# Down projection of a fused transformer block: two halves of an output row accumulated side by side, so that consecutive matmuls name the same stationary tile

## The chip, the cores and the metric

The kernel runs on one core of one Trainium2 chip. The metric is the device time of one execution in microseconds (us). Several executions of each kernel are timed, and medians are given with the lowest and highest run. Executions can fall into a slower state with a lower granted clock; every run on record here is marked as of the fast state (mean granted clock 0.994 to 1.000), so nothing here compares runs of different states.

## The reference

The reference computes one adaptive-layernorm block: linear attention with a residual, then a SwiGLU feed-forward network with a residual. What matters here is its last line, and in it the product with `w_down`.

```python
# x: 1 x 2048 x 1024 (bf16), w_gate and w_up: 1024 x 3584, w_down: 3584 x 1024
def _B_ref(x, w_gate, w_up, w_down):
    g = _silu(x @ w_gate)
    u = x @ w_up
    return g * u @ w_down
...
h = _layernorm(x, axis=-1) * (1 + cb) + sb
x = x + gb * _B_ref(h, B_w_gate, B_w_up, B_w_down)
```

## The kernel before

TensorE (PE) writes its sums to PSUM, which this kernel uses as 8 banks; ScalarE (ACT) and VectorE (DVE) take them out of the banks again, which is called evacuation below. A small scheduler records every operation through a helper and works out the semaphore waits from the buffers that each operation reads and writes. For PSUM it does so by bank. All instructions therefore carry the helper's line number, L178, in the profile, and one reads it by tile names.

The 2048 rows are worked on in four chunks of 512. Each chunk first computes `AT` (3584 x 512, as 28 tiles of 128 partitions), which is the product of gate and up. Then comes the down projection. For each of the four groups of 128 rows (a "row" below), each half of 512 output columns is one sum over the 28 tiles:

```python
# PS: PSUM, 8 banks of 512 fp32 columns. WD(ft): tile ft of w_down (128 x 1024), resident in SBUF.
for j in range(4):
    st = 4 * ch + j
    for nh in range(2):                                  # the two halves of a row of output
        bank = 4 + y_ctr[0] % 2
        i = y_ctr[0] % 2
        y_ctr[0] += 1
        last = (st == NST - 1 and nh == 1)
        parts = [(0, 384, bank), (384, 512, 6)] if last else [(0, 512, bank)]
        for (c0, c1, pb) in parts:
            for ft in range(NFT):                        # NFT = 28
                P.pe("matmul", out=PS[:, pb, c0:c1], lhsT=AT[:, ft, j * 128:(j + 1) * 128],
                     rhs=WD(ft)[:, nh * 512 + c0:nh * 512 + c1], start=(ft == 0), stop=(ft == NFT - 1))
            # evacuation: ACT copies the bank to ATT, DVE multiplies by GB_B, DVE adds to XRES, DMA out
            ...
```

`lhsT` is the stationary operand (128 x 128, loaded into the array by an LDWEIGHTS), and `rhs` is the moving one (512 columns streamed through). In this order the stationary tile changes with every matmul, and each tile of `AT` is loaded twice, 28 matmuls apart. One place in the kernel before already has pairs with equal stationary tiles:

```python
def m_mm(hg, banks):                                     # folds WO with the masked KV matrix
    for nh in range(2):
        ...
        P.pe("matmul", out=PS[:, bank, :], lhsT=KVT[:, hg, :], rhs=WO[:, hg, nh * 512:(nh + 1) * 512],
             start=True, stop=True)
```

## Time and profile before

| what | value | from |
|---|---|---|
| time, median of 3 | 841.77 us (841.69 to 842.76) | the timed runs |
| TensorE (PE) busy | 832.7 of 839.7 us, 99% | first part of the page |
| weight loads (PEld) busy | 384.4 us, 46% | first part of the page |
| first down stage (224 matmuls) | 401.84 - 353.49 = 48.35 us, 215.8 ns each | timeline |
| one weight load | 98 ns | groups by shape |

The first lines of the page. PE is TensorE's matmuls, PEld its weight loads, and PEclk the granted clock in tenths:

```profile
span 839.7 us, 10390 instructions
...
PE 832.7 (99%) x4291; PEld 384.4 (46%) x4291; DVE 296.6 (35%) x627; ACT 211.9 (25%) x363; POOL 39.7 (5%) x51
...
PEclk9999999999999999999999999999999999999999
```

There are as many loads as matmuls, 4291 of each: every matmul brings its own. A busy share of 99% doesn't yet say that PE can't go faster, because the ends of matmuls in the record are modelled and overlap the next. The chain of work that ended last is the stronger evidence. These are its last lines (start, length, what):

```profile
225.05 612.15 PE ps L178 x2877
837.23 0.30 DVE ut L178
837.55 0.22 DVE xres L178
```

For 612.15 us no matmul waited for anything, and the whole down projection lies inside that stretch. Now what sets the pace within it. First the groups by shape (count, busy us, mean ns of one, idle before), for the down projection and for the pairs that share `KVT`:

```profile
L178 PE MATMUL ps<-wd_a,at 128*128 128x512 bf16 x496 | 112.1, 379 | 0.0
L178 PE MATMUL ps<-wd_b,at 128*128 128x512 bf16 x372 | 85.3, 379 | 0.0
...
L178 PEld LDWEIGHTS ps<-wd_a,at 128*128 128x128 bf16 x528 | 51.1, 98 | 59.8
L178 PEld LDWEIGHTS ps<-wd_b,at 128*128 128x128 bf16 x396 | 38.3, 98 | 44.7
...
L178 PEld LDWEIGHTS ps<-wo,kvt 128*128 128x128 bf16 x16 | 1.5, 97 | 2.9 <-ACT mw L178 1.1 <-DVE kvt L178 0.4 <-DVE mw L178 0.2
```

The 379 ns of a matmul is its latency, not its pace. The pace is the distance of starts: 48.35 us / 224 = 215.8 ns. The Trainium skill, page "TensorE: Matmul & The Clock Gate", section "Phases on the wall clock", gives 512 columns at 2.4 GHz, 213 ns, plus a fixed 2.5 ns. The trace agrees, so matmuls already start at the pace that this formula gives for their columns alone, without a term for the load.

A timeline shows where a load is meanwhile. This is the end of the last row but one, and the start of the last row's first sum (start, length, engine, what, count):

```profile
823.79 1.24 PE L178 MATMUL ps<-wd_b,at 128*128 128x512 bf16 x5
824.01 0.53 PEld L178 LDWEIGHTS ps<-wd_b,at 128*128 128x128 bf16 x3
824.66 3.34 PEld L178 LDWEIGHTS ps<-wd_a,at 128*128 128x128 bf16 x16
824.87 3.62 PE L178 MATMUL ps<-wd_a,at 128*128 128x512 bf16 x16
825.15 0.60 ACT L178 ACTIVATE att<-ps 128x512 bf16<-128x512 f32 x1 [5.45 <-PE ps L178]
```

The 16 loads of `wd_a` matmuls start at 824.66, one matmul (0.21 us) before the first matmul that uses one. The 98 ns of a load lie under the 216 ns of the matmul before.

### The profile page before, as it was taken

How to read it: one execution, taken by the hardware profiler on the slowest of the kernel's cores; microseconds unless marked ns; L12 is line 12 of the kernel's file. 1: busy time of each engine (PE TensorE's matmuls, PEld its weight loads, DVE VectorE, ACT ScalarE, POOL GpSimd, SP SyncE). 2: the span in 40 equal slices, each digit the busy share in tenths (PEclk: the TensorE clock that was granted, in tenths of full speed). 3: DMA queues.
4: the chain of work that ended last, by engine and by line, in shares of the span. 5: the costliest groups of instructions: out<-in, count | busy, mean ns of one | idle time of the engine just before them, and what ended most of it. 6: DMA issues, size and time to landing. Idle time of an engine off the chain costs nothing.

```text
span 839.7 us, 10390 instructions
## 1 busy us (share of the span) xinstructions
PE 832.7 (99%) x4291; PEld 384.4 (46%) x4291; DVE 296.6 (35%) x627; ACT 211.9 (25%) x363; POOL 39.7 (5%) x51
## 2 busy tenths in 40 slices
PE   8999999999999999999999999999999999999998
PEld 4444444444444444444444444444444444444444
DVE  4677866656984211111121111122111112111111
ACT  5677763313332111101111111011111011111101
POOL 1000000000050000030000003000000300000000
PEclk9999999999999999999999999999999999999999
DMA  9792323756195895540355552035556203553000
GB/s 311 220 323 51 59 106 126 160 147 249 53 240 179 259 303 155 154 97 25 94 156 153 154 155 67 26 107 150 151 151 157 68 20 107 151 151 99 7 20 26
DMA packets 173391, 113.02 MB, mean 135 GB/s; under 512 B 32536, under 2 KB 156576, under 8 KB 173344
## 3 DMA queue, kind: packets, MB, share of 16 engines
q1 hardware_dynamic: 173344, 112.35, 47.2%
q8 instruction: 34, 0.56, 0.3%
q14 instruction: 13, 0.11, 0.0%
HBM read 100.67 MB, written 4.33 MB: 125 GB/s over the span
## 4 chain that ended last, share of the span: by engine, by line
PE 95%; SPq 2%; DMA 1%; DVE 1%; ACT 0%; issue 0%; ACTq 0%; DVEq 0%
PE ps L178 95%; SPq L178 2%; DMA xres<-in_A_x_dram 1%; DVE acc L178 0%; ACT ht L178 0%; DVE xres L178 0%; DVE mhl L178 0%; DVE stats L178 0%; ACT mw L178 0%; ACT e_92 L178 0%; DVE ve_72 L178 0%; DVE ut L178 0%; DVE mv L178 0%; ACT rl L178 0%; DVE mean_70 L178 0%
## 5 line engine op out<-in xcount | busy, mean ns | idle before, releaser
L178 DVE TENSOR_TENSOR at<-sg,ps 128x512 bf16<-128x512 bf16 x112 | 77.1, 688 | 297.6 <-PE ps L178 297.6
L178 ACT ACTIVATE sg<-ps 128x512 bf16<-128x512 f32 x112 | 67.0, 598 | 310.8 <-PE ps L178 310.8
L178 PE MATMUL ps<-wd_a,at 128*128 128x512 bf16 (+2 forms) x528 | 115.9, 373 | 0.0
L178 PE MATMUL ps<-wd_b,at 128*128 128x512 bf16 (+2 forms) x396 | 88.3, 373 | 0.0
L178 PEld LDWEIGHTS ps<-wd_a,at 128*128 128x128 bf16 x528 | 51.1, 98 | 59.8
L178 DVE TENSOR_TENSOR ut<-att,gb_b 128x512 bf16<-128x512 bf16 (+1 forms) x32 | 14.0, 439 | 165.5 <-ACT att L178 165.5
L178 ACT ACTIVATE att<-ps 128x512 bf16<-128x512 f32 (+1 forms) x32 | 19.0, 594 | 180.0 <-PE ps L178 180.0
L178 PEld LDWEIGHTS ps<-wd_b,at 128*128 128x128 bf16 x396 | 38.3, 98 | 44.7
L178 PE MATMUL ps<-wqk,ht 128*128 128x512 bf16 x256 | 58.4, 382 | 0.1
L178 PE MATMUL ps<-ht,wqk 128*128 128x512 bf16 x256 | 58.4, 383 | 0.0
L178 PE MATMUL ps<-mw,pqt 128*128 128x512 bf16 x256 | 56.2, 379 | 0.1
L178 PE MATMUL ps<-h2t,gug_114 128*128 128x512 bf16 x224 | 52.9, 379 | 0.0
L178 PE MATMUL ps<-h2t,guu_115 128*128 128x512 bf16 x224 | 52.9, 379 | 0.0
L178 PE MATMUL ps<-h2t,gug_112 128*128 128x512 bf16 x224 | 52.9, 379 | 0.0
L178 PE MATMUL ps<-h2t,guu_116 128*128 128x512 bf16 x224 | 52.9, 379 | 0.0
L178 PE MATMUL ps<-h2t,guu_117 128*128 128x512 bf16 x224 | 52.9, 379 | 0.0
L178 PE MATMUL ps<-h2t,guu_118 128*128 128x512 bf16 x224 | 52.9, 379 | 0.0
L178 PE MATMUL ps<-h2t,gug_111 128*128 128x512 bf16 x224 | 52.9, 379 | 0.0
L178 PE MATMUL ps<-h2t,gug_113 128*128 128x512 bf16 x224 | 52.9, 379 | 0.0
L178 POOL TENSOR_SCALAR h2t<-h2t,modcol 128x512 bf16<-128x512 bf16 x32 | 27.0, 863 | 396.8 <-DMA h2t<-xn_119 396.8
L178 ACT ACTIVATE e_92<-ps 128x512 bf16<-128x512 f32 x56 | 33.6, 601 | 27.0 <-PE ps L178 24.5
L178 PEld LDWEIGHTS ps<-mw,pqt 128*128 128x128 bf16 x256 | 24.9, 98 | 29.7 <-DVE xres L178 0.2
(123 smaller groups left out, 708.7 us busy)
## 6 DMA issues: line engine op xcount, KB each, us to landing
gug_111<-in_B_w_gate_dram SPq DMA_DIRECT2D x14, 512.0 KB, 4.0
guu_115<-in_B_w_up_dram SPq DMA_DIRECT2D x14, 512.0 KB, 5.3
gug_112<-in_B_w_gate_dram SPq DMA_DIRECT2D x14, 512.0 KB, 4.0
guu_116<-in_B_w_up_dram SPq DMA_DIRECT2D x14, 512.0 KB, 5.3
gug_113<-in_B_w_gate_dram SPq DMA_DIRECT2D x14, 512.0 KB, 4.0
guu_117<-in_B_w_up_dram SPq DMA_DIRECT2D x14, 512.0 KB, 5.3
gug_114<-in_B_w_gate_dram SPq DMA_DIRECT2D x14, 512.0 KB, 4.0
guu_118<-in_B_w_up_dram SPq DMA_DIRECT2D x14, 512.0 KB, 5.3
```

The lines of the kernel that those rows point to most:

```text
L178: return getattr(e, method)(**kw)
```

## The change

Its intent is to make the two matmuls that use the same tile of `AT` consecutive, so that the tile is loaded once for both, or at least so that the second load costs nothing. For each row, both halves are accumulated side by side in two banks. Because both banks fill until the row's end, the next row takes another pair (banks 4/5 and 6/7 in turn). The last row keeps the old order, so that the tail of the kernel is not longer.

```diff
-        y_ctr = [0]
         out_ops = []
 ...
             for j in range(4):
                 st = 4 * ch + j
+                bb = 4 + 2 * (st % 2)
+                last = st == NST - 1
+                if not last:
+                    for ft in range(NFT):
+                        for nh in range(2):
+                            P.pe("matmul", out=PS[:, bb + nh, :], lhsT=AT[:, ft, j * 128:(j + 1) * 128],
+                                 rhs=WD(ft)[:, nh * 512:nh * 512 + 512], start=(ft == 0), stop=(ft == NFT - 1))
                 for nh in range(2):
-                    bank = 4 + y_ctr[0] % 2
-                    i = y_ctr[0] % 2
-                    y_ctr[0] += 1
-                    last = (st == NST - 1 and nh == 1)
-                    parts = [(0, 384, bank), (384, 512, 6)] if last else [(0, 512, bank)]
+                    i = nh
+                    parts = [(0, 384, bb + 1), (384, 512, 4)] if last and nh == 1 else [(0, 512, bb + nh)]
                     for (c0, c1, pb) in parts:
-                        for ft in range(NFT):
-                            P.pe("matmul", out=PS[:, pb, c0:c1], ...)
+                        if last:
+                            for ft in range(NFT):
+                                P.pe("matmul", out=PS[:, pb, c0:c1], ...)
                         # evacuation: unchanged but for one condition, equal in effect (cut)
```

## The prediction

> **What bounds the kernel now.** TensorE. The page's first part gives PE 832.7 of 839.7 us (99%); the chain of waits ends in 612.15 us of PE from 225.05 us on without one wait, and the down projection lies wholly inside it. In the table of stretches the first down stage (353.49 to 401.84 us, 224 matmuls of 512 columns) takes 48.35 us, 215.8 ns per matmul; gate/up has the same pace (16 matmuls start 3.45 us apart in the timeline). The granted clock is 1.00 in both. The down projection is thus about 193 us, 23% of the span.
>
> **What binds within a matmul.** Streaming the 512 columns, not loading weights. The groups by shape show each LDWEIGHTS at 98 ns beside matmuls 216 ns apart; in the timeline the loads run one matmul ahead, and no idle time of PE is booked to them. The Trainium skill, "TensorE: Matmul & The Clock Gate", section "Phases on the wall clock", puts the gap of back-to-back 512-column matmuls at 215.7 ns; the trace agrees (215.8). So a load is already free.
>
> **What the change removes.** Perhaps nothing. Two consecutive matmuls now name the same tile of AT, but each is still a matmul with its own stationary operand. The kernel before has such pairs: where WO is folded with the masked KV matrix, two consecutive matmuls share KVT and go to different banks. The groups show 16 loads for these 16 matmuls: none was dropped for being equal. In the timeline the pair at 180.63 us starts 0.43 us before the next matmul, 215 ns each: neither slower nor faster for equal tiles or alternating banks. I expect still 924 loads in the down projection, 98 ns each, hidden. If the 15 x 28 = 420 duplicate loads did vanish, weight-load busy time would fall by about 41 us, all under running matmuls: worth 0 on the path. Even if the 2.5 ns above pure streaming (512 columns at 2.4 GHz by the same page) went for every second matmul, that would be 1 us.
>
> **What it moves.** Same DVE, ACT and DMA instructions in the same order, no new waits there (the comparison of orders shows only PE changed). A row's two halves end 0.2 us apart instead of 6 us, so evacuations come in pairs every 12.1 us. A pair costs ACT 2 x 0.60 and DVE 4 x 0.43 us. Bank pairs alternate (4/5, 6/7), so the next row never waits. At the end of the first three chunks two halves are evacuated while gate/up starts; its first Silu comes 1.7 us later and the first multiply 3.5 us later, so the extra 0.6 us of ACT and 0.9 us of DVE fit. Outputs bunch in pairs; DMA is only 25% busy there. The last row keeps the old order, so the tail (837.2 to 839.7 us) stays.
>
> **Prediction.** 841.7 us, range 840.3 to 843.3; chances: faster by over 2% 0.01, within 2% 0.98, slower 0.01.
>
> **What would show each step.** Down stages still 48.3 us per 224 matmuls; LDWEIGHTS of the two WD groups still 528 and 396; ACT's copies and DVE's products in pairs; no PE idle between rows or at the start of the next gate/up; last row's timeline as before.
>
> **What would make it wrong.** The second load of an equal tile can't be pulled ahead (up to 98 ns on 420 matmuls, +41 us), which the 180.63 us pair speaks against; alternating banks over long runs cost something that 16 matmuls don't show; or waits at the three chunk boundaries (under 2 us each).

## The result, and the profile after

| kernel | median of 4 | lowest to highest | ratio to before, 95% interval |
|---|---|---|---|
| before | 841.73 us | 840.85 to 842.76 | |
| after | 841.40 us | 840.67 to 842.44 | 0.9997 (0.9979 to 1.0014) |

A ratio here is the mean time of one kernel's fast runs over that of the other's of the same rounds, so it is not quite the ratio of the medians. The time is the same. A second, longer measurement on another chip (run x1_after_again below) gives 1.0003 (0.9989 to 1.0016).

The page of the changed kernel:

```profile
span 839.5 us, 10310 instructions
...
PE 827.5 (99%) x4211; PEld 384.3 (46%) x4291; DVE 295.9 (35%) x627; ACT 210.2 (25%) x363; POOL 41.3 (5%) x51
```

There is a trap here. PE shows 5.2 us less busy time than before, which looks like a gain. But it also shows 4211 matmuls against 4291 loads. The program has 4291 matmuls, and 80 records are missing from this trace, also in parts of the kernel that the change doesn't touch. The profile of the same kernel in run x1_after_again has all of them:

```profile
PE 832.9 (99%) x4291; PEld 384.4 (46%) x4291; DVE 296.2 (35%) x627; ACT 210.3 (25%) x363; POOL 41.2 (5%) x51
```

So busy time is 832.9 us, the same as before. The last lines of the chain in that profile:

```profile
225.51 612.15 PE ps L178 x2877
837.69 0.30 DVE ut L178
838.01 0.23 DVE xres L178
```

The stretch without a wait is 612.15 us, equal to that of the kernel before in the last digit. The span differs by 0.4 us because this stretch began 0.46 us later (225.51 instead of 225.05), before anything that was changed. The loads of the changed kernel, from its own profile:

```profile
L178 PEld LDWEIGHTS ps<-wd_a,at 128*128 128x128 bf16 x528 | 51.1, 98 | 59.8
L178 PEld LDWEIGHTS ps<-wd_b,at 128*128 128x128 bf16 x396 | 38.3, 98 | 44.6
```

Not one load went away: 528 + 396 = 924 as before, 98 ns each. A matmul instruction of this program brings a load, whether or not its tile was just loaded. And the row change, answering to the timeline before:

```profile
819.54 5.34 PE L178 MATMUL ps<-wd_b,at 128*128 128x512 bf16 x23
824.50 3.33 PEld L178 LDWEIGHTS ps<-wd_a,at 128*128 128x128 bf16 x16
824.72 3.62 PE L178 MATMUL ps<-wd_a,at 128*128 128x512 bf16 x16
824.78 1.08 ACT L178 ACTIVATE att<-ps 128x512 bf16<-128x512 f32 x2 [10.98 <-PE ps L178]
```

The only thing that moved is the evacuation. ACT now copies two banks together every 12 us, instead of one every 6 us. The next row's matmuls start before the copies do and don't wait, because they go to the other pair of banks.

### The profile page after: what moved, and what is told of

Its sections match the earlier page's. It is cut to its first block, busy times and chain, and to the rows that moved or that the text cites. A ratio compares the mean times of both kernels' runs of the same rounds, so it can differ in the third digit from the quotient of the medians.

```text
span 839.5 us, 10310 instructions
## 1 busy us (share of the span) xinstructions
PE 827.5 (99%) x4211; PEld 384.3 (46%) x4291; DVE 295.9 (35%) x627; ACT 210.2 (25%) x363; POOL 41.3 (5%) x51
## 4 chain that ended last, share of the span: by engine, by line
PE 94%; SPq 2%; DMA 1%; DVE 1%; issue 1%; ACT 0%; DVEq 0%; ACTq 0%
PE ps L178 94%; SPq L178 2%; DMA xres<-in_A_x_dram 1%; DVE acc L178 0%; ACT ht L178 0%; DVE xres L178 0%; DVE mhl L178 0%; DVE stats L178 0%; ACT mw L178 0%; ACT e_92 L178 0%; DVE ve_72 L178 0%; ACT rl L178 0%; DVE ut L178 0%; DVE mv L178 0%; DVE mean_70 L178 0%
## 5 line engine op out<-in xcount | busy, mean ns | idle before, releaser
L178 DVE TENSOR_TENSOR at<-sg,ps 128x512 bf16<-128x512 bf16 x112 | 77.0, 687 | 296.2 <-PE ps L178 285.1
L178 ACT ACTIVATE sg<-ps 128x512 bf16<-128x512 f32 x112 | 66.9, 597 | 310.3 <-PE ps L178 298.9
L178 PE MATMUL ps<-wd_a,at 128*128 128x512 bf16 (+2 forms) x519 | 112.8, 372 | 0.5
L178 PE MATMUL ps<-wd_b,at 128*128 128x512 bf16 (+2 forms) x388 | 85.4, 372 | 0.5
L178 PEld LDWEIGHTS ps<-wd_a,at 128*128 128x128 bf16 x528 | 51.1, 98 | 59.8
L178 DVE TENSOR_TENSOR ut<-att,gb_b 128x512 bf16<-128x512 bf16 (+1 forms) x32 | 13.9, 434 | 167.3 <-ACT att L178 167.3
L178 ACT ACTIVATE att<-ps 128x512 bf16<-128x512 f32 (+1 forms) x32 | 17.4, 592 | 182.1 <-PE ps L178 182.1
L178 PEld LDWEIGHTS ps<-wd_b,at 128*128 128x128 bf16 x396 | 38.3, 98 | 44.6
L178 PE MATMUL ps<-ht,wqk 128*128 128x512 bf16 x248 | 57.8, 386 | 0.8 <-ACT rl L178 0.4
L178 PE MATMUL ps<-wqk,ht 128*128 128x512 bf16 x250 | 57.0, 379 | 0.5
L178 PE MATMUL ps<-mw,pqt 128*128 128x512 bf16 x250 | 55.8, 379 | 0.4
L178 PE MATMUL ps<-h2t,guu_117 128*128 128x512 bf16 x221 | 52.8, 379 | 0.2
L178 PE MATMUL ps<-h2t,guu_115 128*128 128x512 bf16 x219 | 52.6, 379 | 0.3
L178 PE MATMUL ps<-h2t,gug_114 128*128 128x512 bf16 x220 | 52.6, 379 | 0.2
L178 PE MATMUL ps<-h2t,guu_116 128*128 128x512 bf16 x221 | 52.6, 379 | 0.2
L178 PE MATMUL ps<-h2t,gug_111 128*128 128x512 bf16 x220 | 52.5, 379 | 0.2
L178 PE MATMUL ps<-h2t,gug_112 128*128 128x512 bf16 x219 | 52.5, 379 | 0.2
L178 PE MATMUL ps<-h2t,gug_113 128*128 128x512 bf16 x219 | 52.3, 379 | 0.3
L178 PE MATMUL ps<-h2t,guu_118 128*128 128x512 bf16 x217 | 52.1, 379 | 0.3
L178 POOL TENSOR_SCALAR h2t<-h2t,modcol 128x512 bf16<-128x512 bf16 x32 | 28.6, 911 | 395.8 <-DMA h2t<-xn_119 395.8
L178 ACT ACTIVATE e_92<-ps 128x512 bf16<-128x512 f32 x56 | 33.6, 600 | 27.0 <-PE ps L178 24.5
L178 PEld LDWEIGHTS ps<-mw,pqt 128*128 128x128 bf16 x256 | 24.9, 98 | 29.7 <-DVE xres L178 0.2
```

The costliest lines, as they stand in the source:

```text
L178: return getattr(e, method)(**kw)
```

## The experiments

The theory (A): the pace of the down projection is set by streaming 512 columns, and a load is hidden whether or not its tile is new. A null result alone doesn't show this, and these are the rivals. (B) Equal tiles do save something, and the alternating banks or the paired evacuation cost as much. (C) There is a small gain, lost in noise. (D) The 2.5 ns above pure streaming is the price of taking over a new tile, and it would go if the duplicate load were really dropped (the 2.5 ns are the fixed term of the page's formula above; the narrower matmuls of x5 and x7 show it too). Nine kernels were run; all gave correct results. The runs of one chip share their runs of the kernel before.

For the runs at the same pace there is a measure much finer than the total time. It is the distance from the start of the last unbroken stretch of matmuls (225.05 us in the kernel before) to the start of the kernel's last group of matmuls (12 of 128 columns, 836.36 us). It leaves out the start of the kernel, where the total time gets much of its scatter. Before: 836.36 - 225.05 = 611.31 us.

| run | ratio to before, 95% interval | from the last stretch's start to the last group | loads |
|---|---|---|---|
| before | | 836.36 - 225.05 = 611.31 us | 4291 |
| x1_after_again | 1.0003 (0.9989 to 1.0016) | 836.82 - 225.51 = 611.31 us | 4291 |
| x2_one_load | 1.0000 (0.9987 to 1.0012) | 837.30 - 226.00 = 611.30 us | 3871 |
| x3_banks_only | 0.9997 (0.9984 to 1.0009) | 835.80 - 224.49 = 611.31 us | 4291 |
| x4_two_loads | 1.0000 (0.9986 to 1.0013) | 836.25 - 224.95 = 611.30 us | 5131 |

### x1_after_again: the changed kernel, timed longer

No edit.

> The changed kernel once more, timed on the same chip as the next runs. Theory A (streaming the 512 columns sets the pace, and a weight load is hidden whether its tile is new or not): within 0.2% of the kernel before, 840 to 843 us, 924 loads in the down projection at 98 ns. Rival B (equal tiles save a little and the alternating banks or paired evacuations give it back): the same here, so this run only sets the base for the next two. Rival C (a small gain was lost in the noise of four runs): 0.1 to 0.3% faster with an interval that excludes 1.

Measured: 842.38 us median of 5 against 842.28 of 9 runs of before. The interval includes 1, and in the trace the distance of the table is 611.31 us in both. C falls: there is no gain of even 0.1 us in the part that was changed, in the one execution of each that was traced.

### x2_one_load: the duplicate load really dropped

The second matmul of each pair is built as an instruction that carries no load of its own:

```diff
+        def pe_noload(out, lhsT, rhs, start, stop):
+            op = P.pe("matmul", out=out, lhsT=lhsT, rhs=rhs, start=start, stop=stop)
+            def fn(e):
+                return e.add_instruction(mybir.InstMatmult(..., ldweights=False,
+                    ins=[e.lower_ap(rhs), e.lower_ap(lhsT)], outs=[e.lower_ap(out)]))
+            op.fn = fn
 ...
                         for nh in range(2):
-                            P.pe("matmul", out=PS[:, bb + nh, :], ...)
+                            mm = pe_noload if nh == 1 else lambda **kw: P.pe("matmul", **kw)
+                            mm(out=PS[:, bb + nh, :], ...)
```

> The changed kernel with the second matmul of each pair issued without a weight load of its own, so that the 420 duplicate loads are really gone (3871 loads in the program for 4291 matmuls). Theory A: weight-load busy time falls by about 420 x 98 ns = 41 us (from 384 to 343 us), the time stays within 0.2% of the kernel before, down stages still 48.35 us per 224 matmuls. Rival D (the about 2.5 ns per matmul above pure streaming is the price of taking over a new tile): 420 x 2.5 ns = 1.05 us less (0.12%), down stages 47.9 us. A rival that takes loads to be on the path would have up to 41 us less. The result must stay correct, which shows that the tile of the first matmul of a pair is still in the array for the second.

Measured: 841.78 us median of 5, correct. The page:

```profile
PE 832.2 (99%) x4291; PEld 343.3 (41%) x3871; DVE 296.5 (35%) x627; ACT 210.4 (25%) x363; POOL 41.2 (5%) x51
```

And the timeline at a row's end, where 390.70 is the first matmul of the next row (L178 is a matmul with a load, L1012 one without):

```profile
390.27 0.38 PE L178 MATMUL ps<-wd_b,at 128*128 128x512 bf16 x1
390.48 0.38 PE L1012 MATMUL ps<-wd_b,at 128*128 128x512 bf16 x1
390.48 0.10 PEld L178 LDWEIGHTS ps<-wd_a,at 128*128 128x128 bf16 x1 [0.33 <-issue]
390.70 0.38 PE L178 MATMUL ps<-wd_a,at 128*128 128x512 bf16 x1
```

This is what the change was after. 420 loads are gone, 41.1 us of load time with them (384.4 to 343.3), and the matmuls still start 0.21 to 0.22 us apart with or without a load. The stretch of the table is 611.30 us. D falls: 420 x 2.5 ns would have been 1.05 us there, and the difference is 0.01 us. The matmul without a load gives the right sums, although the next tile's load starts beside it (390.48).

### x3_banks_only: alternating banks, meant to have no equal tiles (the edit missed this)

```diff
-                    for ft in range(NFT):
+                    for k in range(NFT):
                         for nh in range(2):
-                            ... start=(ft == 0), stop=(ft == NFT - 1))
+                            ft = (k + nh) % NFT
+                            ... start=(k == 0), stop=(k == NFT - 1))
```

> The changed kernel with the second half's sum shifted by one tile (28 tiles, cyclically), so banks alternate and evacuations come in pairs as in the change, but no two consecutive matmuls share a stationary tile. Theory A: same as the changed kernel within 0.2%. Rival B: the cost of the alternation without the saving of equal tiles, so slower than the changed kernel by as much as equal tiles had saved (0.1% or more).

Measured: 841.76 us median of 5, the distance of the table 611.31 us. But the edit doesn't do what the expectation says. With the second half shifted by one tile, the tiles of a row come in the order 0, 1, 1, 2, 2, 3, and so on: the second matmul of one step and the first of the next name the same tile. So 27 of a row's 28 equal pairs are still there, only across the banks in the other order. This run is the change once more in effect, and it can't speak against B.

The kept traces of x1 and of before settle B instead, by the starts of the single matmuls, which the traces hold to the nanosecond (the timeline view merges them). In x1 every matmul of the paired rows goes to another bank than the one before it, but only every second one finds its tile just used. The 420 matmuls with an equal tile start 215.87 ns after the one before on average, the 405 with a new tile (inside a row) 215.80 ns. In the kernel before, where every tile is new and the bank stays the same through a half, the matmuls at the same places start 215.86 and 215.80 ns after the one before. So an equal tile saves nothing, and going to another bank costs nothing. The first matmul of each next row of a chunk starts 215 or 216 ns after the last of the row before in both, so the paired evacuation costs PE nothing either. B falls by this, not by x3.

### x4_two_loads: one extra load before each matmul

```diff
                         for nh in range(2):
+                            P.pe("ldweights", weights=AT[:, ft, j * 128:(j + 1) * 128])
                             P.pe("matmul", out=PS[:, bb + nh, :], ...)
```

> The changed kernel with one extra weight load (the same tile) before each of the 840 full matmuls of the down projection: the suspected cost doubled. Theory A: 2 x 98 ns is still less than the 216 ns of a matmul, so the time stays within 0.3% (840 to 843.5 us), and weight-load busy time rises by about 82 us. If loads can't be queued two deep ahead of a running matmul (only one tile can wait), the extra load is exposed in part: up to 98 ns x 840 = 82 us more. Either way it shows how much slack a load has.

Measured: 841.68 us median of 4, the distance of the table 611.30 us. The page, and the timeline at a matmul:

```profile
PE 831.5 (99%) x4291; PEld 417.3 (50%) x5131; DVE 296.2 (35%) x627; ACT 210.3 (25%) x363; POOL 41.1 (5%) x51
```

```profile
353.39 0.10 PEld L178 LDWEIGHTS <-at 128*128 128x128 bf16 x1
353.43 0.10 PEld L178 LDWEIGHTS ps<-wd_a,at 128*128 128x128 bf16 x1
353.58 0.69 DVE L178 TENSOR_TENSOR at<-sg,ps 128x512 bf16<-128x512 bf16 x1 [2.76 <-PE ps L178]
353.60 0.10 PEld L178 LDWEIGHTS <-at 128*128 128x128 bf16 x1
```

The time is as expected: loads can be doubled for nothing. The expected 82 us more of load time is wrong, it rose by 33 us (384.4 to 417.3). The reason is in the timeline: the second load starts 0.04 us after the first, so the two loads of 96 to 97 ns overlap. A load's 98 ns is a latency too.

### x8_eight_loads: seven extra loads before each matmul

```diff
+                            for _ in range(7):
+                                P.pe("ldweights", weights=AT[:, ft, j * 128:(j + 1) * 128])
```

> Seven extra loads before each of the 840 full matmuls. The fourth run showed two loads 40 ns apart and no time lost. 8 x 40 = 320 ns is over the 216 ns of a matmul: if loads are paced at 40 ns and are executed in order ahead of their matmul, the pace becomes about 320 ns (up to 340 with the last load's own time partly exposed), 840 x 104 to 124 ns = 87 to 104 us more, 929 to 946 us. If it stays at 842 us, equal loads cost less than 27 ns each. The result must be correct.

Measured: 909.44 us median of 2, ratio 1.080 (1.078 to 1.082). A row's first matmuls:

```profile
353.70 0.34 PEld L178 LDWEIGHTS <-at 128*128 128x128 bf16 x7
...
353.99 0.10 PEld L178 LDWEIGHTS ps<-wd_a,at 128*128 128x128 bf16 x1
354.00 0.34 PEld L178 LDWEIGHTS <-at 128*128 128x128 bf16 x7
```

This is the control: here loads do set the pace, and the trace shows it. Each matmul takes 0.30 us. The first down stage is 420.08 - 353.69 = 66.39 us, / 224 = 296 ns per matmul, instead of 215.8, and 840 x 80.6 ns = 67.7 us is the 67.2 us between the medians. Seven loads that take 0.34 us together start (0.34 - 0.096) / 6 = 41 ns apart. So the expected pace (320 to 340 ns) was a little high: eight loads take 296 ns, 37 ns each. By this the threshold lies where loads in a row last longer than 216 ns. At 37 ns a load that is an estimated five to six loads per 512-column matmul (215.8 / 37 = 5.8; no run tried five or six), and the kernel has one. The number of instructions is not what binds: x8 takes 9 of them in 296 ns, 33 ns each, while x6 below gets through a load and a matmul in 29 ns. The extra loads all name the tile of the matmul after them, so the 37 ns are measured for equal tiles.

### x5_n128_all_loads, x6_n64_all_loads, x7_n64_one_load: would it pay with narrower matmuls?

The full matmuls are cut into pieces of 128 columns (x5) or 64 (x6, x7), so that consecutive equal tiles are plentiful (8 or 16) and there is less streaming to hide a load. In x5 and x6 every piece has its load; in x7 only the first of sixteen.

```diff
                         for nh in range(2):
-                            P.pe("matmul", out=PS[:, bb + nh, :], ...)
+                            for c in range(0, 512, 64):          # x5: 128
+                                P.pe("matmul", out=PS[:, bb + nh, c:c + 64], ..., start=(ft == 0 and c == 0), ...)
+                                # x7: without a load unless nh == 0 and c == 0
```

> The changed kernel with each of the 840 full matmuls of the down projection cut into four of 128 columns, each with its own load: eight consecutive matmuls now have equal stationary tiles, and each has only 128 columns of streaming to hide a 98 ns load. The last row of the kernel before has such matmuls already, 16 within 0.89 us, 55.6 ns each, and the extra loads of the fourth run started 40 ns apart. Theory A: loads overlap each other too and stay hidden: 4 x 55.6 - 215.8 = 6.6 ns more for each 512 columns, 840 x 6.6 = 5.5 us more, 847 us. Rival (the load's 98 ns is a floor of the pace once streaming is shorter): 4 x 98 - 215.8 = 176 ns x 840 = 148 us more, 990 us.

> As the run before, with pieces of 64 columns: eight matmuls for each 512 columns, each with a load. If loads are paced at 40 ns, as the extra loads of the fourth run were, the load sets the pace: 8 x 40 - 215.8 = 104 ns x 840 = 88 us more, 929 us. If loads in a stream of matmuls are paced at 25 ns, as in the kernel before where 128x1 matmuls start 25 ns apart, streaming still sets it (64 columns at 128 columns per 53 ns, plus 2.5 ns, 29 ns): 8 x 29.2 - 215.8 = 18 ns x 840 = 15 us more, 857 us.

> Pieces of 64 columns with one load for each sixteen consecutive matmuls of equal tile. Loads can't bind here. Streaming at 29.2 ns each: 15 us more than before, 857 us. If it is as slow as the run with all loads, then what slows narrow matmuls is not the loads; if it is far faster than that run, sharing a tile pays there, and the change would have paid with narrow matmuls.

Measured against 842.24 us of before: x5 847.67 us (ratio 1.0062, 1.0045 to 1.0079), x6 865.72 us (1.028, 1.026 to 1.030), x7 856.01 us (1.016, 1.014 to 1.018).

x5 is the 5.4 us slower that the narrower streaming explains, so 98 ns loads stay hidden under 128-column matmuls 56 ns apart. x7 is 13.8 us slower where 15 were expected. The three widths also show the two terms of the pace that the expectations use: 215.8 ns at 512 columns, 55.8 at 128 (x5: 403.99 - 353.96 = 50.03 us for 896 pieces) and 29.2 at 64 (x7, below) lie on a line of 0.4167 ns per column (53.3 ns per 128) plus 2.5 ns. x6 lies between its two stories, 9.7 us slower than x7. Two lines of the timeline of x6 tell how:

```profile
353.31 1.57 PEld L178 LDWEIGHTS ps<-wd_a,at 128*128 128x128 bf16 x45
353.53 1.45 PE L178 MATMUL ps<-wd_a,at 128*128 128x64 bf16 x44
...
361.50 0.69 PE L178 MATMUL ps<-wd_a,at 128*128 128x64 bf16 x18 [0.89 <-issue]
```

Within a burst, matmuls start (1.45 - 0.193) / 43 = 29 ns apart, each with its load. That is also the pace of x7, whose first stage of 1792 pieces took 405.96 - 353.69 = 52.27 us, 29.2 ns each. So even there a load in a stream of matmuls costs no pace. What x6 loses lies mostly in a few gaps, 6.6 us of PE idle in 5 places, for which the profile names no releaser ("issue"); from the start of the last matmul before to the next one, they cost 7.4 us. x7, with 6300 loads fewer, has no such gap. The other 1.6 us by which the two traces differ follow the longest gap (3.1 us idle, to 516.25 us): from 516.20 to 519.60 us the mean granted clock is 0.54 in x6, and some 60 matmuls start 53 ns apart. The profiled runs are 8.8 us apart, a little less than the medians. Why PE had nothing to do in the gaps is not shown. Each of them ends 1.2 to 1.5 us after a packet of the instruction queue has landed, and x6 has 79 such packets where x7 has 55; this points to instructions that came late, but most such packets come without a gap, and no run tests it.

### x9_two_banks: are the two extra banks needed?

```diff
-                bb = 4 + 2 * (st % 2)
+                bb = 4
```

> The changed kernel with banks 4 and 5 for every row instead of the alternating pairs 4/5 and 6/7: what the two extra banks of the change are worth, and whether the paired evacuation has a cost that they hide. In the changed kernel's trace the last two rows meet like this: the next row's first matmul starts at 824.72 us, the two copies out of the banks run from 824.78 to 825.86. With the same banks, the next row's second sum could start only after 825.86 instead of at 824.94: about 1 us of waiting of PE at each of the 12 row changes inside a chunk (between chunks gate/up lies in between), 11 to 15 us in all with the restart, so 853 to 857 us, PE idle booked to ACT. If it stays at 842 us, the pairs of banks were not needed and my reading of the evacuation is wrong.

Measured: 852.52 us median of 4, ratio 1.0129 (1.0112 to 1.0146). A row change:

```profile
365.14 1.08 ACT L178 ACTIVATE att<-ps 128x512 bf16<-128x512 f32 x2 [12.92 <-PE ps L178]
365.79 0.10 PEld L178 LDWEIGHTS ps<-wd_a,at 128*128 128x128 bf16 x1 [0.97 <-ACT att L178]
365.79 4.54 PE L178 MATMUL ps<-wd_a,at 128*128 128x512 bf16 x19 [0.47 <-ACT att L178]
...
366.27 3.78 PEld L178 LDWEIGHTS ps<-wd_a,at 128*128 128x128 bf16 x19 [0.39 <-ACT att L178]
```

The next row waits for the two copies: the first down stage takes 404.33 - 353.07 = 51.26 us, 2.91 us more than before, for its three row changes. That is 0.97 us each, as expected, and 11.6 us for twelve at most, since the kernel's last row needs only one bank at first. The medians are 10.3 us apart, and the ratio gives 10.9 us; the time is just under the expected 853 to 857 us. So the changed order does have a cost. It holds both banks to the row's end and evacuates them together, and the alternating pairs of banks hide that.

## Why the prediction was right

- **What binds.** It said streaming, 215.8 ns per matmul, and down stages of 48.3 us. After: 402.30 - 353.95 = 48.35 us for the first (x1_after_again). With the loads halved in pairs (x2) or doubled (x4) the unbroken stretch keeps its length within 0.01 us; with eight loads per matmul (x8) the pace rises to 296 ns. This shows that the kernel is on the streaming side, with one load where an estimated five to six would fit.
- **What the change removes.** It said perhaps nothing, and that 924 loads would remain. All 924 remain, 98 ns each. The reading of the 16 loads for the 16 `KVT` matmuls in the trace before was the right evidence: the program had already tried the change on a small scale.
- **If the loads did vanish.** It said 41 us less load time, worth 0, or 1 us if the 2.5 ns went. x2 measured 41.1 us less and 0.01 us on the path, so the 2.5 ns isn't paid for a new tile.
- **What it moves.** Evacuations come in pairs, ACT takes 1.08 us for two (the prediction's 2 x 0.60 was slightly high), no row waits, and the tail is unchanged: from the start of the last matmul group to the last addition it is 837.55 - 836.36 = 1.19 us before and 838.01 - 836.82 = 1.19 us after. At a chunk boundary the second half's addition ends at 404.67 us in x1, 1.3 us ahead of the first product of gate and up at 405.95, as foreseen. x9 shows that the two extra banks are what makes this free.
- **The dangers it named** (a second load that can't be pulled ahead; alternating banks) are ruled out by x1: 611.31 us as before, and 215.8 to 215.9 ns from matmul to matmul with equal and with new tiles.

Several sizes in the expectations of runs were off, none of them in the prediction: the load time of x4 (33 us more, not 82, because loads overlap each other), the pace of x8 (296 ns, not 320 to 340), the time of x6 (the gaps) and, barely, that of x9. And x3 was not the kernel that its expectation describes.

## What to carry to other kernels

Before removing an operation, look up what it runs under: here a weight load started a whole matmul ahead and took 98 ns under 216 ns of streaming, and removing 420 of the 924 changed the path by 0.01 us. When a reordering yields nothing, check three things apart before calling it useless: that the saving took place at all (count the instructions), that it was on the path (remove it for real), and that nothing was paid back (do the reordering without the saving, or compare single steps with and without it). And write out the first few steps of a control before it runs: x3 kept the equal pairs that it was to remove. If two sums are accumulated side by side, give the next pair its own banks; here that was worth 10 us.

## What the Trainium skill lacked or had wrong

- "TensorE: Matmul & The Clock Gate", section "Back-to-back issue gap", gives a sustained roofline for a stream of load and matmul pairs of about 131 ns per matmul at 512 columns and 81 ns at 128. Here such streams run at 215.8 ns and 56 ns (x5); it is the page's "isolated" formula that holds, also with a load for every matmul.
- The same page, "LDWEIGHTS (loading the stationary operand)", gives P / 1.2, 107 ns for 128 columns. The record is 96 to 98 ns, but that is a latency: loads one after the other start 41 ns apart (x8), and loads between 64-column matmuls 29 ns apart (x6), which is the pace of those matmuls without loads too (x7). For a stream of loads this interval matters and not the latency, and the section doesn't give it.
- The same page, "The mechanism", says in its list of what overlaps that loads overlap matmuls in flight only if their row groups differ. A sentence before it in that section also lets loads to a background weight buffer go ahead, so the list is too narrow by the page itself. Here loads of the full 128 x 128 array start one matmul (0.21 us) ahead of the matmul that uses them, under the matmul before, throughout.
- "Perfetto Trace Analysis", section "Identifying the Most-Contended Engine", offers the busy share of LDWEIGHTS, beside the share of peak FLOPs, as a measure of how close TensorE is to its limit. The former was 41%, 46% and 50% in three kernels of the same time (x2, after, x4), so it said nothing about the limit here.
- No page says that equal consecutive stationary tiles don't merge (924 loads before and after), or what dropping the load by hand is worth (0.01 us for 420 loads at 512 columns).
